# Routing by scattered token numbers, early blocks and one dispatch per expert in a linear-attention and expert kernel

## The chip, the cores and the metric

The kernel runs on one core of one Trainium2 chip. Its metric is the device time of one execution in microseconds (us). The engines are PE (matmul), DVE (vector), ACT (scalar), POOL (general purpose, and issuer of the indirect DMAs) and SP (issuer of plain DMAs). Each works through its own queue of instructions in order; semaphores order the queues against each other.

## The reference

A gated linear attention is followed by a mixture of eight experts, of which each token uses one.

```python
# attention: B, H, S, D = 4, 8, 768, 48, float32
for t in range(S):
    state = alpha[:, :, t, :, None] * state + np.einsum('bhd,bhde->bhde', k[:, :, t], v[:, :, t])
    y[:, :, t] = np.einsum('bhd,bhde->bhe', q[:, :, t], state)
x = y.transpose(0, 2, 1, 3).reshape(B * S, H * D)            # N = 3072 rows of 384
# router
xn = x / (norm(x) + 1e-6); en = expert_emb / (norm(expert_emb) + 1e-6)
logits = xn @ en.T / tau                                     # E = 8
expert_idx = np.argmax(logits, axis=1)
probs = softmax(logits)                                      # sum + 1e-9
gate_w = probs[np.arange(N), expert_idx]
# experts: w1 [8, 384, 1024], w2 [8, 1024, 384]
out[mask_e] = gate_w[mask_e, None] * (np.maximum(x[mask_e] @ w1[e], 0) @ w2[e])
```

## The kernel before

**Attention.** The 3072 tokens are 24 chunks of 128 (six for each of the four batches). The loop at the end of the attention part is written as a pipeline: in iteration s it loads chunk s + 2, takes the decays of chunk s (transposes on PE, two scans on DVE, `qs` on POOL), the scores of chunk s - 1, the mixing of chunk s - 2 and the rows of chunk s - 3. The function `rows` multiplies the transposed result with a selection matrix that also holds the expert embeddings, so that one PSUM tile `px` has a chunk's 384 values of x and its eight logits; ACT copies x out, DVE sums the logits, SP stores the 128 rows in the DRAM tensor `x_rows`, and ACT forms the sum of squares. The programs for the engines are put in order by a scheduler that follows the order of the program where an operation is ready, and it adds the waits. Each read of a tile or DRAM tensor waits for the writes that come before it in the program and touch the same part.

**Choosing an expert.** After each batch, `choose` scales the logits of six chunks (a square root and an exponential on ACT, eleven operations on DVE), marks the winning expert in `chosen` and adds up on POOL how often each expert was chosen before each chunk (`before`).

**Routing.** When the attention is over, the part with the lines 404 to 490 places all tokens at once: two matmuls rank every token within its expert (`rk`), DVE turns the ranks into a block number and a row, 24 matmuls of one-hot matrices (`in_row`, `inv`) invert that into the token number and the gate for each row of 31 possible blocks, and further DVE operations give the indices for gathering and scattering (`gidx`, `sidx`), each block's expert (`eblk`) and whether its weights have to be loaded (`fresh`).

**Experts.** `block` (line 506) handles 128 rows of one expert: it loads the expert's w1 and w2 into one of two buffers unless the block two before had the same expert, gathers the 128 rows of x with an indirect DMA (line 526), turns them with three PE transposes (536), runs the first layer as 24 matmuls with 128 moving columns (545) and ACT's ReLU, the second as 8 matmuls with 384 moving columns (555), multiplies by the gate on DVE (559) and scatters the rows to the output (560). A float32 matmul shows as two records in the profile, so that a block has 48 and 16 of them. Every expert's rows are filled up to whole blocks. The first 24 blocks are straight code. How many there are in all is known only at run time, so the last blocks are the arms of one dispatch (`Switch`, line 577): every engine loads the count into a register (`values_load`, line 573) and branches to its code of that arm. Each arm begins with a hint for its exit branch.

Of the kernel before, what the change touches and what calls it, by code (L numbers as in the profile page):

```python
# [9 lines left out]
FP32 = mybir.dt.float32  # L10
# [5 lines left out]
SP = mybir.EngineType.SP  # L16

# [6 lines left out]
def kernel(  # L24
# [24 lines left out]

    NBLK = (N + E * (P - 1)) // P  # L50
    FAR = 1 << 20

    x_rows = nc.dram_tensor("x_rows", (N, DM), FP32, kind="Internal").ap()
# [12 lines left out]
    zeros = consts.tile([P, P], FP32)  # L66
    nc.gpsimd.memset(zeros, 0.0)
    cols_i = consts.tile([P, P], I32)
    nc.gpsimd.iota(cols_i, pattern=[[1, P]], base=0, channel_multiplier=0)
    cols = consts.tile([P, P], FP32)  # L70
    nc.vector.tensor_copy(cols, cols_i)
    toks_i = consts.tile([P, NS], I32)
    nc.gpsimd.iota(toks_i, pattern=[[P, NS]], base=1, channel_multiplier=1)
    toks = consts.tile([P, NS], FP32)
    nc.vector.tensor_copy(toks, toks_i)
    first = consts.tile([P, E], FP32)
    nc.vector.tensor_scalar(first, cols[:, 0:E], -1.0, float(E), ALU.mult, ALU.add)


    lg = consts.tile([P, NS, E], FP32)  # L80
    sq = consts.tile([P, NS], FP32)
    gate = consts.tile([P, NS], FP32)
    chosen = consts.tile([P, NS, E], FP32)
    before = consts.tile([P, NS + 1, E], FP32)
    nc.gpsimd.memset(before[:, 0], 0.0)
    rtau = consts.tile([P, 1], FP32)
    gidx = consts.tile([P, NBLK], I32)
    sidx = consts.tile([P, NBLK], I32)
    bgate = consts.tile([P, NBLK], FP32)
    eblk = consts.tile([1, NBLK], I32)  # L90
    fresh = consts.tile([1, NBLK], I32)
    nmore = consts.tile([1, 1], I32)


    with ExitStack() as c1:
# [7 lines left out]
        NBUF, NBV = 4, 6  # L103
# [33 lines left out]
        sel = pads.tile([P, NP, 2 * D + E], FP32, name="sel")  # L137

        al0 = pads.tile([P, NP, NS], FP32, name="al0")

        def prepare():
# [15 lines left out]
            nc.vector.reciprocal(en, en)  # L157
            embp = work.tile([E, H, DP], FP32, name="embp", bufs=1)
# [23 lines left out]
        def choose(b):  # L182
            s0, s1 = b * NCH, (b + 1) * NCH
            shp = [P, NCH, E]
            l = lg[:, s0:s1]
            rn = work.tile([P, NCH], FP32, name="rn")
            nc.scalar.activation(rn, sq[:, s0:s1], AF.Sqrt)
            nc.vector.tensor_scalar(rn, rn, 1e-6, None, ALU.add)
            nc.vector.reciprocal(rn, rn)
            nc.vector.tensor_scalar(rn, rn, rtau, None, ALU.mult)  # L190
            nc.vector.tensor_tensor(l, l, bc(rn, shp, 2), ALU.mult)
            top = work.tile([P, NCH], FP32, name="top")
            nc.vector.tensor_reduce(top.unsqueeze(2), l, axis=AX.X, op=ALU.max)  # L193
            win = work.tile(shp, FP32, name="win")
            nc.vector.tensor_tensor(win, l, bc(top, shp, 2), ALU.is_equal)
            nc.vector.tensor_tensor(win, win, bc(first, shp, 1), ALU.mult)
            best = work.tile([P, NCH], FP32, name="best")
            nc.vector.tensor_reduce(best.unsqueeze(2), win, axis=AX.X, op=ALU.max)
            nc.vector.tensor_tensor(chosen[:, s0:s1], win, bc(best, shp, 2), ALU.is_equal)
            for s in range(s0, s1):  # L200
                nc.gpsimd.tensor_tensor(before[:, s + 1], before[:, s], chosen[:, s], ALU.add)
            sh = work.tile(shp, FP32, name="sh")
            nc.vector.tensor_tensor(sh, l, bc(top, shp, 2), ALU.subtract)
            nc.scalar.activation(sh, sh, AF.Exp)
            g = gate[:, s0:s1]
            nc.vector.tensor_reduce(g.unsqueeze(2), sh, axis=AX.X, op=ALU.add)
            nc.vector.tensor_scalar(g, g, 1e-9, None, ALU.add)
            nc.vector.reciprocal(g, g)
# [153 lines left out]
        def rows(s):  # L362
# [3 lines left out]
            for p in range(NP):  # L366
                nc.tensor.matmul(px[:, p], lhsT=yT[:, p], rhs=sel[:, p], start=True, stop=True)  # L367
            x = work.tile([P, NP, 2 * D], FP32, name="x", bufs=3)
            nc.scalar.copy(x, px[:, :, 0 : 2 * D])
            nc.vector.tensor_reduce(  # L370
                lg[:, s].unsqueeze(2), px[:, :, 2 * D :].rearrange("t p e -> t e p"),
                axis=AX.X, op=ALU.add,
            )
            xf = x.rearrange("t p d -> t (p d)")
            nc.sync.dma_start(out=x_rows[s * P : (s + 1) * P], in_=xf)
            x2 = work.tile([P, DM], FP32, name="x2")
            nc.scalar.activation(x2, xf, AF.Square, accum_out=sq[:, s : s + 1])
            if s % NCH == NCH - 1:
                choose(s // NCH)
# [22 lines left out]


    with ExitStack() as c2:
        rt = c2.enter_context(tc.tile_pool(name="rt", bufs=1))
        ps_rt = c2.enter_context(tc.tile_pool(name="ps_rt", bufs=1, space=PSUM))


        rk = ps_rt.tile([P, (NS + 1) * E], FP32, name="rk")
        nc.tensor.matmul(  # L410
            rk, lhsT=ones, rhs=before.rearrange("p s e -> p (s e)"), start=True, stop=False
        )
        nc.tensor.matmul(
            rk[:, 0 : NS * E], lhsT=earlier, rhs=chosen.rearrange("p s e -> p (s e)"),
            start=False, stop=True,
        )

        nb_i = rt.tile([P, E], I32, name="nb_i")
# [74 lines left out]
    with ExitStack() as c3:  # L493
# [77 lines left out]
        for j in range(NS):  # L571
            block(j)
# [37 lines left out]
```

## Time and profile before

| | us |
|---|---|
| median of three runs | 535.98 (533.46 to 536.34) |
| the profiled execution | 535.62 |
| its span, first to last instruction | 533.9 |
| PE busy, DVE busy | 464.1, 182.4 |
| last `px` of the attention ends | 162.0 |
| first expert matmul | 206.9 |
| last expert matmul ends | 523.8 |

The page of the profile has 40 equal slices of the span (13.3 us each), in which a digit is the busy share of an engine in tenths; PEclk is the clock that PE was granted, again in tenths. The chain of waits follows the work that ended last back through the program. A group line gives a line of the kernel, engine, operation, operands and shapes, then the number of instructions, their busy time, the mean of one in ns, and the idle time before them with what ended it. In a timeline the columns are start, duration, engine, line, operation. In the view of one source line, a name such as PEldq is the sequencer of that engine, the numbers after the count are the shortest, the median and the longest in ns, and then come the first and the last start.

### The profile page before, as it was taken

The numbers are of one execution on the slowest core, as the hardware profiler recorded it, in microseconds if no ns is written. First come the engines' busy times: TensorE is split into PE (matmuls) and PEld (weight loads), VectorE is DVE, ScalarE is ACT, GpSimd is POOL, SyncE is SP. The second block draws the span as 40 slices with busy tenths as digits, with TensorE's granted clock in tenths as the row PEclk, the third lists the DMA queues.
The fourth block names the chain that finished last, engine by engine and source line by source line (L and its number), as shares of the span: only waits on it lengthen the run. The fifth ranks groups of instructions, "written<-read, shape, count | busy, mean of one in ns | idle before, by whom it ended". The sixth has DMA issues, their size and how long they took to land.

```text
span 533.9 us, 9347 instructions
## 1 busy us (share of the span) xinstructions
PE 464.1 (87%) x3677; PEld 387.4 (73%) x3677; DVE 182.4 (34%) x391; ACT 111.2 (21%) x214; POOL 139.2 (26%) x224
## 2 busy tenths in 40 slices
PE   2999999999992636999999999999999999964992
PEld 2899889899891625778777787877778777743871
DVE  5888998998974710100101111010110101001000
ACT  2244544645543000101110001100001100000110
POOL 6554544553430132001202022020220200102000
PEclk9999999999997556999999999999999999995997
DMA  9889778777000078038477384086159295582000
GB/s 188 170 179 199 168 151 173 159 152 163 31 32 29 1 269 321 16 119 291 142 260 270 134 293 152 30 301 219 46 205 319 60 321 173 180 301 84 16 18 16
DMA packets 130229, 84.78 MB, mean 159 GB/s; under 512 B 102095, under 2 KB 121595, under 8 KB 130168
## 3 DMA queue, kind: packets, MB, share of 16 engines
q1 hardware_dynamic: 126336, 73.93, 48.2%
q0 software_dynamic: 3456, 10.03, 5.1%
q8 instruction: 32, 0.52, 0.4%
q14 instruction: 29, 0.24, 0.1%
q10 hardware_dynamic: 376, 0.05, 0.1%
HBM read 109.17 MB, written 10.03 MB: 223 GB/s over the span
## 4 chain that ended last, share of the span: by engine, by line
PE 73%; issue 10%; DVE 9%; DMA 4%; POOL 1%; another core or an unknown queue 1%; ACT 1%; POOLq 0%; ACTq 0%; DVEq 0%
PE ph L545 25%; PE pyo L555 23%; PE sc L328 4%; PE px L367 4%; PE py L342 3%; PE py L354 3%; DMA xg<-x_rows,gidx 2%; PE pkb L277 2%; PE inv L460 2%; PE pa L216 2%; PE pd L305 2%; DVE r L246 2%; PE pq L216 1%; PE pk L216 1%; DVE y L559 1%
## 5 line engine op out<-in xcount | busy, mean ns | idle before, releaser
L545 PEld LDWEIGHTS ph<-xgT,w 128*128 128x128 f32 x1296 | 150.9, 195 | 11.9 <-DVE xgT L538 4.9
L545 PE MATMUL ph<-xgT,w 128*128 128x128 f32 x1296 | 152.8, 279 | 5.5 <-DVE xgT L538 3.4
L555 PE MATMUL pyo<-w,hT 128*128 128x384 f32 x432 | 143.8, 486 | 0.0
L555 PEld LDWEIGHTS pyo<-w,hT 128*128 128x128 f32 x432 | 80.0, 190 | 50.1
L559 DVE TENSOR_SCALAR y<-pyo,bgate 128x384 f32<-128x384 f32 x27 | 16.7, 618 | 263.6 <-PE pyo L555 263.6
L551 ACT ACTIVATE hT<-ph 128x512 f32<-128x512 f32 x54 | 32.2, 597 | 320.5 <-PE ph L545 303.0
L560 POOL DMA_INDIRECT out_dram<-y,sidx x27 | 27.0, 1000 | 187.1 <-DVE y L559 184.7
L526 POOL DMA_INDIRECT xg<-x_rows,gidx x27 | 27.9, 1033 | 105.7 <-PE pxg L536 77.8
L268 POOL TENSOR_TENSOR qs<-qc,a 128x512 f32<-128x512 f32 x24 | 30.6, 1274 | 48.9 <-DVE a L260 30.9
L536 PE MATMUL pxg<-ident,xg 128*128 128x128 f32 x81 | 14.8, 319 | 27.3 <-DMA xg<-x_rows,gidx 18.8
L536 PEld LDWEIGHTS pxg<-ident,xg 128*128 128x128 f32 x81 | 10.9, 162 | 33.3 <-issue 30.5
L332 DVE TENSOR_TENSOR sm<-sc,causal 128x512 f32<-128x512 f32 x48 | 30.6, 674 | 0.5 <-PE sc L328 0.4
L246 DVE TENSOR_TENSOR_SCAN r<-pa,inr 128x511 f32<-128x511 f32 x24 | 29.3, 1220 | 3.6 <-PE pa L216 3.1
L260 DVE TENSOR_TENSOR_SCAN a<-pa,ini 128x512 f32<-128x512 f32 x24 | 29.4, 1223 | 1.2
L328 PE MATMUL sc<-qs,kr 64*128 64x128 f32 x384 | 28.6, 289 | 0.0
L538 DVE COPY xgT<-pxg 128x384 f32<-128x384 f32 x27 | 14.1, 551 | 41.7 <-PE pxg L536 23.3
L328 PEld LDWEIGHTS sc<-qs,kr 64*128 64x128 f32 x384 | 24.0, 192 | 4.1 <-issue 1.9
L289 POOL TENSOR_TENSOR dec<-state,end 64x256 f32<-64x256 f32 x40 | 24.4, 609 | 7.0 <-DVE top L193 1.9
L367 PE MATMUL px<-sel,yT 128*128 128x104 f32 x192 | 25.3, 275 | 0.7 <-ACT yT L360 0.7
L354 PE MATMUL py<-sm,vt 128*64 128x128 f32 x384 | 25.3, 274 | 0.0
L367 PEld LDWEIGHTS px<-sel,yT 128*128 128x128 f32 x192 | 23.3, 192 | 1.3 <-ACT yT L360 0.9
L360 ACT COPY yT<-py 128x512 f32<-128x512 f32 x24 | 14.1, 586 | 37.8 <-PE py L354 37.8
(127 smaller groups left out, 391.9 us busy)
## 6 DMA issues: line engine op xcount, KB each, us to landing
w<-in_moe_w_dram SPq DMA_DIRECT2D x54, 1536.0 KB
at<-in_alpha_dram SPq DMA_DIRECT2D x24, 192.0 KB
kt<-in_k_dram SPq DMA_DIRECT2D x24, 192.0 KB
qt<-in_q_dram SPq DMA_DIRECT2D x24, 192.0 KB
vt<-in_v_dram SPq DMA_DIRECT2D x24, 192.0 KB
x_rows<-x SPq DMA_DIRECT2D x24, 192.0 KB
xg<-x_rows,gidx POOLq DMA_INDIRECT x27, 4.6
out_dram<-y,sidx POOLq DMA_INDIRECT x27, 6.1
```

What stands on the lines that cost most here:

```text
L246: nc.vector.tensor_tensor_scan(r[:, L - 2 :: -1], pa[:, L - 1 : 0 : -1], inr[:, L - 2 :: -1], 1.0, ALU.mult, ALU.add,)
L260: nc.vector.tensor_tensor_scan(a, pa, ini, 0.0, ALU.mult, ALU.add)
L268: nc.gpsimd.tensor_tensor(qs.rearrange("p n t -> p (n t)"), qc, a, ALU.mult)
L328: nc.tensor.matmul(sc[:, hh, p], lhsT=kr[sl, p], rhs=qs[sl, p], start=True, stop=True)
L332: nc.vector.tensor_tensor(sm[:, hh], sc[:, hh], causal.to_broadcast([P, NP, P]), ALU.mult)
L354: nc.tensor.matmul(py[DP * hh : DP * hh + DP, p], lhsT=vt[:, 2 * p + hh], rhs=sm[:, hh, p], start=("dec" not in d and p == 0), stop=True, ...
L367: nc.tensor.matmul(px[:, p], lhsT=yT[:, p], rhs=sel[:, p], start=True, stop=True)
L526: nc.gpsimd.indirect_dma_start(out=xg, out_offset=None, in_=x_rows, in_offset=bass.IndirectOffsetOnAxis(ap=gidx[:, j : j + 1], axis=0), bo ...
L545: nc.tensor.matmul(ph[:, f], lhsT=w1_t[:, i, (f0 + f) * P : (f0 + f + 1) * P], rhs=xgT[:, i], start=(i == 0), stop=(i == KT - 1),)
L551: nc.scalar.activation(hT[:, f0 : f0 + 4], ph, AF.Relu)
L555: nc.tensor.matmul(py, lhsT=hT[:, f], rhs=w2_t[:, f], start=(f == 0), stop=(f == FT - 1))
L560: ins = nc.gpsimd.indirect_dma_start(out=out, out_offset=bass.IndirectOffsetOnAxis(ap=sidx[:, j : j + 1], axis=0), in_=y, in_offset=None, ...
```

## The change

- `choose` is replaced by `place`, called after each of seven groups of chunks (5, 5, 5, 5, 2, 1 and 1). It marks the winner from unscaled logits, ranks the group's tokens with two matmuls, and for each chunk scatters 128 token numbers (plus one) with an indirect DMA from POOL into a DRAM tensor `ids`, which has 3072 places per expert and starts with zeros. The whole routing part after the attention goes.
- The logits and the sum of squares are stored with each row of x, 393 values a row, by ACT instead of SP. The gate is computed from them for the gathered rows (`gates`).
- After 20 chunks, `first_expert` takes the first expert that has at least 256 rows. The experts are then done in turn from it. Its first two blocks are done ahead of all others, from token numbers read in `ids` and rows of the first 20 chunks.
- `counts` gives the rest of each expert's rows in halves of 64, and each expert has one dispatch with an arm for 0 to 8 halves, and one with a loop over blocks for more. In an arm the first layer takes all rows of the expert at once as moving columns (up to 512). The second layer of a last half block uses two matmuls with 64 weight columns, which write different halves of a PSUM tile and are added afterwards.
- Within the arm of one expert the rows of the next one are turned, always four blocks. Weights have three buffers, gathered rows three; weights and rows are fetched two experts ahead, before the dispatch.
- The buffers of v go from six to five.

```diff
-    x_rows = nc.dram_tensor("x_rows", (N, DM), FP32, kind="Internal").ap()
+    GROUPS = ((0, 5), (5, 10), (10, 15), (15, 20), (20, 22), (22, 23), (23, 24))
+    S0, EARLY = 20, 2
+    x_rows = nc.dram_tensor("x_rows", (N, ROW), FP32, kind="Internal").ap()
+    ids = nc.dram_tensor("ids", ((E * NB + NB) * P, 1), I32, kind="Internal").ap()
+    id_blocks = ids.rearrange("(j p) one -> p (j one)", p=P)
...
+    def weights(i):
+        e = nc.values_load(
+            turn_i[0:1, i : i + 1], engines=(SP,), min_val=0, max_val=E - 1,
...
+        nc.sync.dma_start(
+            out=w1_s[i % NW], in_=w1_r[ds(e, 1)].rearrange("e p k f -> (e p) k f")
+        )
...
-        NBUF, NBV = 4, 6
+        NBUF, NBV = 4, 5
...
+        def place(g):
+            nc.vector.tensor_reduce(top.unsqueeze(2), l, axis=AX.X, op=ALU.max)
+            nc.vector.tensor_tensor(win, l, bc(top, shp, 2), ALU.is_equal)
+            nc.vector.tensor_tensor(win, win, bc(first, shp, 1), ALU.mult)
+            nc.vector.tensor_reduce(best.unsqueeze(2), win, axis=AX.X, op=ALU.max)
+            nc.vector.tensor_tensor(ch, win, bc(best, shp, 2), ALU.is_equal)
             for s in range(s0, s1):
+                (nc.vector if s == NS - 1 else nc.gpsimd).tensor_tensor(before[:, s + 1], before[:, s], chosen[:, s], ALU.add)
+            rk = ps_mm.tile([P, GMAX, E], FP32, tag="mm", name="rk")[:, 0:n]
+            nc.tensor.matmul(
+                rkf, lhsT=ones, rhs=before[:, s0:s1].rearrange("p s e -> p (s e)"),
+                start=True, stop=False,
+            )
+            nc.tensor.matmul(
+                rkf, lhsT=earlier, rhs=ch.rearrange("p s e -> p (s e)"),
+                start=False, stop=True,
+            )
+            nc.vector.tensor_tensor(at, rk, ch, ALU.mult)
+            nc.vector.tensor_reduce(row.unsqueeze(2), at, axis=AX.X, op=ALU.add)
+            nc.vector.tensor_copy(dest[:, s0:s1], row)
+            for s in range(s0, s1):
+                ins = nc.gpsimd.indirect_dma_start(
+                    out=ids,
+                    out_offset=bass.IndirectOffsetOnAxis(ap=dest[:, s : s + 1], axis=0),
+                    in_=toks[:, s : s + 1],
...
+                tc.declare_no_dep(ins.ins, group="ids", reason="tokens have a row each")
+                tc.add_to_no_dep_group("ids", ins.ins)
...
             nc.vector.tensor_reduce(
+                l.unsqueeze(2), px[:, :, 2 * D :].rearrange("t p e -> t e p"),
                 axis=AX.X, op=ALU.add,
             )
-            nc.sync.dma_start(out=x_rows[s * P : (s + 1) * P], in_=xf)
+            nc.scalar.copy(x[:, LG : LG + E], l)
+            nc.scalar.copy(x[:, 0:DM].rearrange("t (p d) -> t p d", p=NP), px[:, :, 0 : 2 * D])
+            nc.scalar.activation(x2, x[:, 0:DM], AF.Square, accum_out=x[:, SQ : SQ + 1])
+            nc.scalar.dma_start(out=x_rows[s * P : (s + 1) * P], in_=x)
+            if s == s1 - 1:
+                place(g)
+                if s1 == S0:
+                    first_expert()
+                if s1 == NS:
+                    counts()
...
-    with ExitStack() as c2:
...
+        def gates(xg, gate, n):
+            nc.vector.tensor_reduce(top.unsqueeze(2), l, axis=AX.X, op=ALU.max)
+            nc.scalar.activation(rn, xg[:, :, SQ : SQ + 1], AF.Sqrt)
...
+            nc.scalar.activation(sh, sh, AF.Exp)
+            nc.vector.tensor_reduce(gate.unsqueeze(2), sh, axis=AX.X, op=ALU.add)
...
+        def first_layer(w1_t, hT, xT, f, n):
+            ph = ps_h.tile([P, NC * P], FP32, name="ph")[:, 0:n]
+            for i in range(KT):
+                nc.tensor.matmul(
+                    ph, lhsT=w1_t[:, i, f * P : (f + 1) * P], rhs=xT[:, i, 0:n],
+                    start=(i == 0), stop=(i == KT - 1),
+                )
+            nc.scalar.activation(hT[:, f, 0:n], ph, AF.Relu)
...
+        def second_layer(w2_t, hT, t, n, gate, col):
...
+                for f in range(FT // 2):
+                    for i in range(2):
+                        nc.tensor.matmul(
+                            py[i * HALF : (i + 1) * HALF],
+                            lhsT=hT[:, i * FT // 2 + f, t * P : t * P + HALF],
+                            rhs=w2_t[:, i * FT // 2 + f],
+                            start=(f == 0), stop=(f == FT // 2 - 1), skip_group_check=True,
+                        )
+                nc.scalar.copy(y[0:HALF], py[HALF:])
+                nc.vector.tensor_tensor(y[0:HALF], y[0:HALF], py[0:HALF], ALU.add)
+                nc.vector.tensor_scalar(y[0:HALF], y[0:HALF], gate[0:HALF], None, ALU.mult)
+            scatter(y[0:n], col[0:n])
...
+        def rows_of(i, m, ready=None):
+            hT = hp.tile([P, FT, NC * P], FP32, name="hT") if m else None
+            for f in range(FT):
+                if m:
+                    first_layer(w1_t, hT, xT, f, m * HALF)
+                if i + 1 < E and f % 2 == 1:
+                    prepare(i + 1, f // 2)
+            if i + 1 < E:
+                gates(xg_s[(i + 1) % NXG], gt_s[(i + 1) % 2], NC)
+            for t in range((m + 1) // 2):
+                second_layer(
+                    w2_t, hT, t, min(P, m * HALF - t * P), gt[:, t : t + 1],
+                    sidx[:, i, t : t + 1],
+                )
...
+        nc.sync.dma_start(out=etok, in_=id_blocks[:, ds(lead * NB, EARLY)])
+        for i in range(2):
+            weights(i)
+        tokens_of(etok, egidx, esidx, EARLY)
+        for t in range(EARLY):
+            gather(exg[:, t], x_rows[0 : S0 * P], egidx[:, t : t + 1])
+        for t in range(EARLY):
+            turn(exg[:, t], exT[:, :, t * P : (t + 1) * P])
+        gates(exg[:, 0:EARLY], egt[:, 0:EARLY], EARLY)
+        hT = hp.tile([P, FT, NC * P], FP32, name="hT")
+        for f in range(FT):
+            first_layer(w1_s[0], hT, exT, f, EARLY * P)
+        for t in range(EARLY):
+            if t == EARLY - 1:
+                for i in range(E):
+                    nc.sync.dma_start(out=tok[:, i], in_=id_blocks[:, ds(first_block(i), NC)])
...
+                for i in range(2):
+                    gathers(i)
+                for b in range(NC):
+                    prepare(0, b)
+                gates(xg_s[0], gt_s[0], NC)
+            second_layer(w2_s[0], hT, t, P, egt[:, t : t + 1], esidx[:, t : t + 1])
+        for i in range(E):
+            if i + 2 < E:
+                weights(i + 2)
+                gathers(i + 2)
+            count = nc.values_load(
+                halves[0:1, i : i + 1], min_val=0, max_val=2 * NC + 1,
...
+            for m in tc.Switch(count, 2 * NC + 2):
+                if m <= 2 * NC:
+                    rows_of(i, m)
+                else:
+                    many(i)
```

## The prediction

> **What bounds the kernel now.** First the slices of the span and the busy times by stage: is there one bound or several?
>
> ```profile
> PE   2999999999992636999999999999999999964992
> PEclk9999999999997556999999999999999999995997
> ```
>
> ```profile
> core 0: us, PE busy (x) PEld busy (x) DVE busy (x) ACT busy (x) POOL busy (x), PEclk, DMA share, GB/s
> 93.00:130.00 37.00, 36.47 (x460) 33.55 (x459) 33.71 (x66) 19.24 (x40) 19.10 (x35) 1.00 0.77 164
> ...
> 162.00:206.80 44.80, 16.19 (x67) 14.11 (x68) 17.92 (x69) 4.11 (x7) 10.49 (x14) 0.54 0.38 141
> 206.80:475.50 268.70, 263.12 (x1595) 209.03 (x1593) 24.16 (x45) 28.66 (x48) 40.80 (x41) 0.99 0.56 192
> 475.50:490.90 15.40, 2.43 (x10) 1.72 (x11) 1.73 (x3) 0.00 (x0) 4.04 (x4) 0.64 0.52 166
> ```
>
> PE bounds the attention (36.5 of 37 us, DVE close behind with 33.7) and the experts (263 of 269). Between them lie 44.8 us with PE a third busy at half clock, and 15.4 us more open up near the end. The chain of waits says what fills the first hole:
>
> ```profile
> 162.03 0.49 ACT x L369
> ...
> 178.00 10.52 PE inv L460 x48
> ...
> 191.38 6.62 DMA xg<-x_rows,gidx
> ...
> 199.40 6.68 DMA xg<-x_rows,gidx
> ...
> 207.08 6.82 PE ph L545 x48
> 213.90 5.16 PE pyo L555 x16
> 219.06 5.36 PE ph L545 x48
> ```
>
> Routing ends at 189.2, and then PE waits for gathers. The transposes of blocks 1 to 4 stand ahead of block 0's first layer on PE's queue, so that layer starts at 206.9 though block 0's rows were there at 197. The second hole is the one dispatch (Switch) of before; the lines of its source and of its timeline show it:
>
> ```profile
> L573 PEldq TENSOR_LOAD <-nmore x1: 483/483/483, 471.0 to 471.0; - x1
> ```
>
> ```profile
> L577 PEldq BRANCH_PREFETCH_HINT  x1: 50/50/50, 477.7 to 477.7; - x1
> ```
>
> ```profile
> L605 PEldq COMPARE_BRANCH  x2: 342/3078/5814, 471.8 to 519.3; - x2
> ```
>
> ```profile
> 470.13 5.33 PE L555 MATMUL pyo<-w,hT 128*128 128x384 f32 x16
> ...
> 484.37 1.05 POOL L526 DMA_INDIRECT xg<-x_rows,gidx  x1 [7.00 <-DMA xg<-x_rows,gidx]
> ```
>
> PE's sequencer reads the count at 471.00, while 4.45 us of issued matmuls still run (to 475.45), and the branch holds it 5.81 us: the arm's first instruction comes at 477.72. So a dispatch costs PE itself 2.3 us; the other 10 of the hole are POOL's branch (476.93 to 482.60) and gathers issued only behind it. The exit branch took PE 0.34, and its next instruction followed at 0.46.
>
> Costs of one instruction:
>
> ```profile
> L545 PE MATMUL ph<-xgT,w 128*128 128x128 f32 x1296 | 152.8, 279 | 5.5 <-DVE xgT L538 3.4
> L555 PE MATMUL pyo<-w,hT 128*128 128x384 f32 x432 | 143.8, 486 | 0.0
> ...
> L560 POOL DMA_INDIRECT out_dram<-y,sidx x27 | 27.0, 1000 | 187.1 <-DVE y L559 184.7
> L526 POOL DMA_INDIRECT xg<-x_rows,gidx x27 | 27.9, 1033 | 105.7 <-PE pxg L536 77.8
> ```
>
> The means are latencies; in the chain 16 second-layer records take 5.17 us (0.323 each, 0.841 ns a column) and 48 first-layer ones 5.36 (0.112, 0.873 ns a column).
>
> **The attention.** Removed: three calls of choose inside the loop (the fourth is in the hole). The scans of L246 start 8.7, 8.0 and 7.9 us apart there against 5.8 elsewhere: 7.2 us. Added: four calls of place in the loop, each with 8 small DVE operations (0.2 to 0.23 and a gap: 1.9 us, on a nearly full DVE), 4 matmul records behind POOL's adds, and 5 scatters on POOL. Scatters cost what L560 does, 1.0 us at a distance of 1.3: a burst of 6.5 us on an engine in order, with qs (L268) and dec (L289) queued behind it, and PE's scores and DVE's state waiting for those. qs has 1.4 us of slack (ends at 87.8, scores from 89.2) and POOL idles about 2 us a chunk before it; over two chunks they absorb 5.4 and leave 1.1. With 0.5 for the matmuls a place costs 3.5, four of them 14. Bounds: 1.9 each (all POOL work hidden) to 10.7 (6.5 + 1.35 of adds + 1.0 + 1.9, nothing hidden). The logits now reach x by an ACT copy that waits for DVE, and the store moves from SP to ACT's queue (issues of 0.27 to 0.62 us there at the start): ACT is half busy, so 0 to 0.3 us a chunk, taken 0.1, together 2.4. One v buffer fewer costs nothing while loads run two chunks ahead: PE never waits for a load in the attention. Sum: 14 + 2.4 - 7.2 = +9; bounds 0 to +43. The last chunk's px ends at 171 instead of 162.0.
>
> **From there to the first layer.** Now 44.9 us. After: six DVE operations 1.4, rank matmuls 0.6, three operations 0.7; the last scatter, landing 2.6 to 6.1 us after issue (L560's rows), taken 4.0 as the queues are emptier; the read of two id blocks on SP, which depends on every scatter (no size of it is in the trace; from 0 up to a gather's 4.6), taken 2.0; three operations 0.7; two gathers 1.6 to the second's issue, landing 3.0 to 6.6 (L526), taken 4.0; transposes and copy 1.5. Together 16.5 (bounds 11 to 24). The first expert is known three chunks earlier, so weights (3 MB, at the 300 GB/s of the slices 10 us) can be on their way, and hide under these waits; if they queue behind the id read they arrive 5 us after it, still in time. First layer from 187.5.
>
> **The experts.** The reference's inputs give the experts 418, 365, 379, 426, 395, 371, 351 and 367 tokens: 27 blocks before. After 20 chunks expert 0 has 337, so it leads, and the rest is 3, 6, 6, 7, 7, 6, 6, 6 halves: 51 with the four early ones. First layer: 48 records of 64 columns a half at 0.841 ns, 2.585 us, 131.8 (at 0.873 it is 137). Second: 24 full blocks of 5.17, 124.1; three half blocks whose two 64-column matmuls go at once. That they do is seen in the attention: 16 such records (L354) take 1.02 us, 8 full-width ones (L342) 1.09. So 2.6 each, 7.8 (15.5 if not). Transposes: four blocks for every expert, full or not, 32 of 0.41: 13.1 (six records take 0.82). The restart at half clock costs 1.3. Sum 278.1.
>
> **Eight dispatches.** PE's path is load 0.48, registers 0.37, branch 5.81, 0.06: 6.72, less the issued work. The first: 2.3. After a full block, with the exit's 0.46: 2.7, four times. After a half block the same 14 issued matmuls last half as long, 2.25: 4.9, and there the clock falls (in the trace it fell 3.65 and 4.2 us after PE stopped, and the next 48 matmuls took 6.7 to 6.8 instead of 5.4): 6.2, three times. Sum 31.7. Bounds: 0 (a branch of 0.34 would hide under the issued work) to 10.5 each (nothing issued ahead, ACT's exit of 2.4, cold clock). I take the same construct's own row.
>
> The Trainium skill (Advanced Engine Details and Errata, Control Flow Timing) gives about 108 ns for a compare-and-branch; by that the dispatches would cost nothing and the sum below would be 32 lower. Its page Runtime: NRT & Kernel Launch (Instruction fetch mechanics) speaks against the change: a taken branch whose target isn't loaded stalls for a fetch. The 5.81 us row is of that kind, so the measurement decides.
>
> **What is covered.** Id reads for all experts, 8 gathers and expert 0's transposes need 19 us behind the last scatter's landing; the early blocks' work ends 31 behind it. Weights of the expert after next have a body of some 35 us. POOL pays per expert four gathers 5.2, scatters 4, paddings of the DMA counts about 5 (0.72 and a wait each), exit and branch 9: 23 of 35. DVE enters an arm 9.5 us after its last y; the third transposed block needs it 9 to 14 us into the arm. ACT's gates (two table loads, 1.28 each) lie beside the second layer. The end stays 10.1 us.
>
> **The sum.** 187.5 + 278.1 + 31.7 + 10.1 = 507.4; outside the span 535.62 - 533.9 = 1.7: 509.1. The profiled execution (535.62) stands 0.4 below the median shown (535.98), so nothing is added.
>
> **Rivals.**
> Dispatch dominates (slower): every gap goes to the upper bound, 84 instead of 31.7, because PE's issued work no longer covers and weight loads slow the fetch: 561. It decides from 7.3 us a gap on. For: eight cold branches on five engines. Against: PE's own gap was 2.3.
> POOL's bursts bound the attention: +36 instead of +9, 536, no change. For: POOL in order, slack of 1.4. Against: POOL is half busy.
> The early blocks don't wait for the last scatters and run beside the last chunks: 16 earlier, when expert 0's rows become the limit: 493. For: their x rows are cut to the first 20 chunks. Against: the ids they read are one tensor that every scatter writes.
> PE's queue order puts expert 0's transposes ahead of the early first layer, as it did with blocks 1 to 4: the cover is lost, +12: 521.
>
> **How the numbers follow.** Forecast 0.56, dispatch 0.13, bursts 0.10, earlier 0.12, order 0.09. Half a per cent (2.7 us) is about what a measurement can tell from no change. Faster: forecast, earlier, order and a third of bursts, 0.80; same 0.06 from bursts; slower, dispatch and a little of bursts, 0.14. The range goes from the earlier case with a cheaper attention, 487, to where dispatch passes before, 541.
>
> **What would show it.** Right: no inv matmuls; the last px near 171; ph at 256 columns from about 187; 48 ph records in 15.5 us for six halves; PE gaps of 2 to 6 us at eight places. Wrong: gaps over 7 us, DVE or PE waiting for qs and dec after each place by more than 5 us, PE waiting for gathers before an arm's transposes, or the last scatter's landing late.

## The result, and the profile after

The changed kernel takes 599.95 us (median of four, 596.96 to 603.28) against 534.86 for the kernel before on the same chip: a ratio of 1.122, with a 95% interval of 1.114 to 1.129. The prediction was 509.1 with a range of 487 to 541. The profiled execution took 596.96 with a span of 595.2.

By stages (windows that end at the first place, the last `px`, the first `ph`, the transposes of expert 0 ahead of the first dispatch, the last matmul of all, and the end of the span; times busy in us, the count of records in brackets, then the granted clock):

```profile
core 0: us, PE busy (x) PEld busy (x) DVE busy (x) ACT busy (x) POOL busy (x), PEclk, DMA share, GB/s
20.00:56.00 36.00, 34.95 (x440) 32.06 (x436) 31.74 (x56) 14.89 (x36) 18.37 (x30) 1.00 1.23 186
56.00:234.10 178.10, 127.10 (x1366) 116.29 (x1366) 94.96 (x201) 48.71 (x121) 74.85 (x119) 0.85 0.51 79
234.10:256.40 22.30, 2.82 (x13) 1.98 (x11) 4.57 (x29) 2.68 (x6) 3.40 (x4) 0.53 0.47 170
256.40:285.50 29.10, 24.90 (x92) 17.90 (x92) 3.84 (x13) 4.21 (x10) 8.48 (x9) 0.91 0.87 266
285.50:581.90 296.40, 264.20 (x868) 154.70 (x868) 41.95 (x119) 52.95 (x99) 49.33 (x50) 0.95 0.28 90
581.90:595.20 13.30, 0.04 (x1) 0.00 (x0) 0.62 (x1) 0.00 (x0) 0.97 (x1) 0.69 0.04 15
```

Until 56 us PE is full as before. From the first place on it works 127 of 178 us, at a clock of 0.85. The slices of the span show the same as holes behind each of the four places of five chunks:

```profile
PE   2998469849829837087778997979889979989991
PEclk9999869889869978579698999999979979999997
```

Against the kernel before and the prediction (first scan is the first scan of DVE, L246 before and L356 after; it starts at 11.5 to 13.7 us, differently from run to run, so the attention is measured from it):

| us | before | predicted | after |
|---|---|---|---|
| first scan to the end of the last `px` | 150.5 | 159.5 | 220.8 |
| from there to the first first-layer matmul | 44.9 | 16.5 | 22.3 |
| first to last expert matmul | 316.9 | 309.8 | 325.5 |
| last matmul to the end | 10.1 | 10.1 | 13.3 |

Of the 88 us between forecast and result, 61 lie in the attention, 6 in the stage behind it, 16 in the experts and 3 at the end; the first scan came 2 late. What PE waits for in the attention is named by the waits (window 55 to 236 us: engine, line and tile, what was waited for, sum, times, longest):

```profile
PE py L452 <- POOL dec L399: 41.9, 4, 12.9
...
POOL dec L399 <- DMA ids<-toks,dest: 34.4, 3, 12.4
DVE state L427 <- POOL dec L399: 24.7, 3, 11.9
...
PE rk L249 <- POOL before L246: 7.6, 5, 1.8
```

POOL's own sequence behind the first place shows how:

```profile
59.53 1.19 POOL L263 DMA_INDIRECT ids<-toks,dest  x1 [0.95 <-DVE dest L261]
61.02 0.97 POOL L263 DMA_INDIRECT ids<-toks,dest  x1 [0.30 <-issue]
62.30 0.97 POOL L263 DMA_INDIRECT ids<-toks,dest  x1 [0.30 <-issue]
63.57 0.97 POOL L263 DMA_INDIRECT ids<-toks,dest  x1 [0.30 <-issue]
64.85 0.97 POOL L263 DMA_INDIRECT ids<-toks,dest  x1 [0.30 <-issue]
65.83 0.23 POOL L373 TENSOR_TENSOR end<-r,al 128x4 f32<-128x4 f32 x1
65.98 0.63 POOL L399 TENSOR_TENSOR dec<-state,end 64x256 f32<-64x256 f32 x1
78.96 0.61 POOL L399 TENSOR_TENSOR dec<-state,end 64x256 f32<-64x256 f32 x1 [12.34 <-DMA ids<-toks,dest]
79.65 1.28 POOL L378 TENSOR_TENSOR qs<-qc,a 128x512 f32<-128x512 f32 x1
```

The burst of five scatters lasts 6.3 us, as the prediction had it. Then the second of the two `dec` instructions waits 12.3 us for their landing, though it touches neither `ids` nor `dest`. In the trace it waits on the semaphores of all five scatters; the first half, on partitions 0 to 63, waits for none, and the second, which starts at partition 64, does. Why only the second carries them is not shown. In the kernel before the two halves of a chunk run back to back, and the longest wait of either in the loop is 1.8 us, for DVE behind a call of choose:

```profile
93.89 1.29 POOL L289 TENSOR_TENSOR dec<-state,end 64x256 f32<-64x256 f32 x2
```

Behind the waiting half stand `qs` and the mixing matmuls. A scatter takes a median of 10.3 us from issue to landing here.

### The profile page after: what moved, and what is told of

The parts are those of the page before. It is cut to its first block, busy times and chain, and to the rows that moved or that the text cites. A ratio compares the mean times of both kernels' runs of the same rounds, so it can differ in the third digit from the quotient of the medians.

```text
span 595.2 us, 7919 instructions
## 1 busy us (share of the span) xinstructions
PE 462.4 (78%) x2814; PEld 330.2 (55%) x2814; DVE 188.2 (32%) x453; ACT 128.6 (22%) x279; POOL 166.3 (28%) x252
## 5 line engine op out<-in xcount | busy, mean ns | idle before, releaser
L594 PE MATMUL ph<-xT,w 128*128 128x384 f32 (+3 forms) x432 | 148.1, 499 | 32.9 <-issue 19.3
L594 PEld LDWEIGHTS ph<-xT,w 128*128 128x128 f32 x432 | 84.8, 204 | 86.1 <-issue 45.9
L606 PE MATMUL pyo<-w,hT 128*128 128x384 f32 x384 | 125.5, 486 | 0.0
L606 PEld LDWEIGHTS pyo<-w,hT 128*128 128x128 f32 x384 | 72.4, 190 | 48.5
L452 PE MATMUL py<-qs,dec 128*128 128x128 f32 x160 | 26.8, 321 | 41.9 <-POOL dec L399 41.9
L610 DVE TENSOR_SCALAR y<-pyo,gt 128x384 f32<-128x384 f32 x24 | 14.8, 618 | 132.4 <-PE pyo L606 132.3
L598 ACT ACTIVATE hT<-ph 128x384 f32<-128x384 f32 (+3 forms) x72 | 31.9, 472 | 77.9 <-PE ph L594 77.8
L452 PEld LDWEIGHTS py<-qs,dec 128*128 128x128 f32 x160 | 23.8, 229 | 43.7 <-POOL dec L399 42.9
L532 POOL DMA_INDIRECT xg<-x_rows,gidx x32 | 32.2, 1006 | 33.5 <-issue 17.4
L571 DVE COPY xT<-pxg 128x384 f32<-128x384 f32 x34 | 18.2, 549 | 58.0 <-PE pxg L570 57.9
L356 DVE TENSOR_TENSOR_SCAN r<-pa,inr 128x511 f32<-128x511 f32 x24 | 29.3, 1220 | 6.7 <-PE pa L326 6.7
L263 POOL DMA_INDIRECT ids<-toks,dest x24 | 23.7, 986 | 14.9 <-DVE dest L261 6.1
## 6 DMA issues: line engine op xcount, KB each, us to landing
x_rows<-x ACTq DMA_DIRECT2D x24, 196.5 KB, 11.5
```

The costliest lines, as they stand in the source:

```text
L356: nc.vector.tensor_tensor_scan(r[:, L - 2 :: -1], pa[:, L - 1 : 0 : -1], inr[:, L - 2 :: -1], 1.0, ALU.mult, ALU.add,)
L452: nc.tensor.matmul(py[:, p], lhsT=dec[:, p].rearrange("p j e -> p (j e)"), rhs=d["qs"][:, p], start=(p == 0), stop=False, skip_group_check ...
L532: nc.gpsimd.indirect_dma_start(out=xg, out_offset=None, in_=src, in_offset=bass.IndirectOffsetOnAxis(ap=col, axis=0), bounds_check=src.sha ...
L594: nc.tensor.matmul(ph, lhsT=w1_t[:, i, f * P : (f + 1) * P], rhs=xT[:, i, 0:n], start=(i == 0), stop=(i == KT - 1),)
L598: nc.scalar.activation(hT[:, f, 0:n], ph, AF.Relu)
L606: nc.tensor.matmul(py, lhsT=hT[:, f, t * P : (t + 1) * P], rhs=w2_t[:, f], start=(f == 0), stop=(f == FT - 1),)
```

## Experiments

The expectations call 236 us the last `px` of the changed kernel; that is the end of the routing's last matmul, and the `px` itself ends at 234.1. Ratios are to the kernel before on the same chip, with 95% intervals.

| run | median us | ratio | first scan to last px | px to first layer | experts |
|---|---|---|---|---|---|
| changed kernel | 599.95 | 1.122 (1.114 to 1.129) | 220.8 | 22.3 | 325.5 |
| dec_one_op | 578.21 | 1.075 (1.069 to 1.082) | 192.2 | 19.9 | 330.9 |
| one_scatter_a_chunk | 573.67 | 1.068 (1.062 to 1.074) | 192.2 | 22.6 | 331.5 |
| scatters_late | 587.32 | 1.097 (1.093 to 1.100) | 167.9 | 60.9 | 328.0 |
| ids_64_bytes | 546.52 | 1.020 (1.016 to 1.025) | 171.0 | 16.0 | 330.8 |
| ids_64_bytes_two_dec | 554.53 | 1.033 (1.028 to 1.037) | 179.6 | 16.4 | 332.1 |
| ranks_one_chunk_later | 530.87 | 0.991 (0.988 to 0.994) | 163.9 | 19.1 | 324.3 |
| norm_in_attention | 519.35 | 0.970 (0.968 to 0.973) | 160.4 | 17.8 | 311.6 |

### The wait of dec

```diff
-            for hh in range(2):
-                sl = slice(DP * hh, DP * hh + DP)
-                nc.gpsimd.tensor_tensor(
-                    dec[sl, :, hh], carried["state"][sl],
-                    d["end"][sl].to_broadcast([DP, NP, DP]), ALU.mult,
-                )
+            shp = [P, NP, 2, DP]
+            nc.gpsimd.tensor_tensor(
+                dec, bc(carried["state"], shp, 2), bc(d["end"], shp, 3), ALU.mult,
+            )
```

`end` gets a second column per head pair, with a factor `al1` that is zero for the other half of the partitions.

> The changed kernel with one edit: dec is computed by one POOL instruction on 128 partitions (its factor end holds zeros for the other half) instead of two on 64, so that no POOL instruction of the attention starts at partition 64, and dec no longer waits for the landing of earlier scatters. The scatters, their number and their place in POOL's order stay. Theory (dec's wait for the landing is the loss): the four gaps of PE before the mixing matmuls (12.9, 6.1, 12.5, 10.4 us, 41.9 together) shrink to 3 or less each, and with them the stretches at half clock (54.6 us in the attention), so that the last px ends at 170 to 185 us instead of 236, and the time is 535 to 555. Rival (five scatters in a row hold POOL, or their traffic holds the other transfers): the gaps move to qs or to the next memset but stay, the last px ends after 220 and the time is 580 to 600.

Measured: 578.21 us, the last `px` at 205.6. The attention loses 28.6 us (220.8 to 192.2), and the waits for the scatters' landing are gone. But both theories missed: the stage is still 33 us above the forecast, and the wait has another form. Two views of the trace show it, first POOL's longest wait from 20 to 206 us, then SP's issues behind the first place (start, duration):

```profile
POOL at L342 <- DMA at<-in_alpha_dram: 37.0, 8, 8.0
```

```profile
62.82 0.37 SPq L340 DMA_DIRECT2D at<-in_alpha_dram  x1
63.67 0.38 SPq L343 DMA_DIRECT2D kt<-in_k_dram  x1
64.15 3.68 SPq L344 DMA_DIRECT2D qt<-in_q_dram  x1
67.93 5.86 SPq L345 DMA_DIRECT2D vt<-in_v_dram  x1
73.89 2.17 SPq L340 DMA_DIRECT2D at<-in_alpha_dram  x1
76.15 4.17 SPq L343 DMA_DIRECT2D kt<-in_k_dram  x1
```

While scatters are on their way SP needs 3.7 and 5.9 us to issue one load of 192 KB (0.4 to 1.5 between 56 and 150 us in the kernel before). The alpha loads are late, and the memset of `at`, which stands in POOL's queue ahead of `dec`, waits for them. So the scatters slow the loads too.

> The kernel before with the same edit of dec alone, as a control. Two instructions of 0.61 us become one like qs (128x512, 1.27 us), so the edit by itself should be worth 0: 533 to 538 by the theory and by the rival. Faster by 10 us or more would mean that the edit removes something else than a wait for scatters.

Measured: 537.65 us, ratio 1.004 (1.001 to 1.007). Inside what was expected: the edit alone brings nothing without scatters; it costs 2 us.

### Scatters outside the attention

```diff
-            for s in range(s0, s1):
+        def send():
+            nc.vector.tensor_copy(dest2, dest)
+            for s in range(NS):
                 ins = nc.gpsimd.indirect_dma_start(
                     out=ids,
-                    out_offset=bass.IndirectOffsetOnAxis(ap=dest[:, s : s + 1], axis=0),
+                    out_offset=bass.IndirectOffsetOnAxis(ap=dest2[:, s : s + 1], axis=0),
...
                 if s1 == NS:
+                    send()
                     counts()
```

> The changed kernel with all 24 scatters issued after the last group's row numbers (they read a copy of these, made there), none in the attention. What is left of place in the loop is the marking, the adding up, the rank matmuls and the logits' way into x. Theory: the last px ends at 165 to 185 us as in the run with one dec instruction, because without scatters nothing is waited for; the scatters then lie bare behind it, 24 x 1.3 = 31 us instead of 1.3, so the first layer starts 45 to 55 us behind the last px and the time is 560 to 580. If place's other parts are the loss (rank matmuls, ACT's copy that waits for DVE), the last px still ends after 215 and the time passes 600.

Measured: 587.32 us. The last `px` ends at 181.3, as expected without any wait for scatters. So marking, ranks and the logits' new way into x cost 167.9 - 150.5 = 17.4 us, net of what the removal of choose gives back. The time itself was missed because the scatters took longer than their issue. Here they run with next to no other traffic (the rate of all DMA in that time rounds to 0 GB/s); the read of the early ids (`etok`, on SP) waits for the last landing:

```profile
184.36 1.18 POOL L267 DMA_INDIRECT ids<-toks,dest  x1 [4.59 <-DVE halves L318]
185.85 0.97 POOL L267 DMA_INDIRECT ids<-toks,dest  x1 [0.30 <-issue]
...
199.94 0.96 POOL L267 DMA_INDIRECT ids<-toks,dest  x1 [1.68 <-DMA ids<-toks,dest]
...
219.65 0.97 POOL L267 DMA_INDIRECT ids<-toks,dest  x1 [0.30 <-issue]
```

```profile
230.84 0.39 SPq L691 DMA_DIRECT2D etok<-ids  x1
```

From 184.4 to 230.8 that is 46.4 us for 24 scatters of 512 bytes, 1.9 us each, though POOL can issue one in 1.27.

### Spread, or wider

Two theories for the slow loads: the burst of five, or the small writes themselves.

```diff
+        later = {S0: (15, 16), S0 + 1: (17, 18), S0 + 2: (19,)}
+        for j in range(S0 - 5):
+            later[j + 5] = (j,)
...
+            for j in later.get(s, ()):
+                send(j, s)
```

> The run with one dec instruction, with the scatters of a group of five spread over the next five chunks, one a chunk (the row numbers of a chunk are rounded by a small DVE instruction in the later chunk; the last groups as before), so that no more than two follow each other. Theory C (it is the burst of five in a row that holds POOL 6.5 us and starves the loads): one scatter of 1.3 us fits into POOL's idle 2 us a chunk, the waits of the memset for alpha fall below 12 us, the last px ends at 181 to 190 instead of 206, and the time is 545 to 558. Rival D (every scatter takes its 2 to 4 us from the loads wherever it stands): the loads are late a little in each chunk, the last px ends at 198 to 210 and the time stays at 565 to 585.

Measured: 573.67 us, with the last `px` at 205.8: rival D. Spreading moves the waits (19.2 us of the memset for alpha, 24.6 us of the rank matmuls for POOL's adds, 9.6 the longest) and gains nothing in the attention.

```diff
-    ids = nc.dram_tensor("ids", ((E * NB + NB) * P, 1), I32, kind="Internal").ap()
+    ids = nc.dram_tensor("ids", ((E * NB + NB) * P, W), I32, kind="Internal").ap()    # W = 16
...
-                    in_=toks[:, s : s + 1],
+                    in_=toks_w[:, s],                  # the token number 16 times
```

> The run with one dec instruction, with places of 64 bytes instead of 4 in ids: each scatter writes 128 pieces of 64 bytes (16 copies of the token number, of which the first is read), and the zeros at the start are nine DMAs of 197 KB. In the run with all scatters late, 24 of them took 46.4 us from the first issue to the last landing with no other traffic (1.9 us each for 0.5 KB, while POOL could issue one in 1.27). Theory A (writes of 4 bytes are what is slow, and what slows the loads beside them): the waits of POOL's memset for the alpha load (37 us with 4 bytes) fall below 12, the last px ends at 183 to 193 instead of 206, and the time is 545 to 560. Rival B (any indirect DMA of 128 pieces beside the loads costs the same): the waits stay above 25 us, the last px ends at 200 to 210, the time stays at 570 to 585.

Measured: 546.52 us, the last `px` at 182.7: theory A. Five scatters in a row are still there, and cost 171.0 - 167.9 = 3.1 us against none in the loop. The loads behind the first place are issued in 0.4 to 1.1 us, the memset waits 0.8 us in all, and the DMA list (55 to 200 us; median time to landing last) has:

```profile
x_rows<-x ACTq DMA_DIRECT2D x19, 196.5 KB, 3.2
ids<-xg,dest POOLq DMA_INDIRECT x24, 2.2
```

In the changed kernel's list the same two stand at 15.5 and 10.3 us:

```profile
x_rows<-x ACTq DMA_DIRECT2D x15, 196.5 KB, 15.5
ids<-toks,dest POOLq DMA_INDIRECT x15, 10.3
```

The 64-byte places alone, with `dec` left in two instructions:

> The changed kernel with places of 64 bytes in ids as its only edit; dec stays two instructions, of which the second still waits for the landing of the group's five scatters. Theory (scatters of 4 bytes are the cause, dec's wait only one of the ways in which their slowness reaches PE): with landings of 2.2 us, as in the run with 64 bytes and one dec, the wait costs POOL about 2 us a group, 4 groups 8 at most; the last px ends at 183 to 192 us and the time is 546 to 557. Rival (dec's wait costs by itself, however fast the scatters are): four gaps of 6 us or more stay at PE's mixing matmuls, the last px ends after 205 and the time is 570 or more.

Measured: 554.53 us, the last `px` at 191.5. The wait of `dec` is worth 8.6 us (179.6 - 171.0) when scatters land in 2.2 us, and 28.6 when they take 10. It carries the slowness of the scatters to PE; it isn't the root.

### Size of a write, or its neighbours

A chunk's tokens of one expert get places next to each other, so with 4-byte places up to 16 writes of one scatter fall into the same 64 bytes.

```diff
-                    in_=toks_w[:, s],
+                    in_=toks[:, s : s + 1],            # ids is flat again, dest times 16
```

> The run with one dec instruction and places of 64 bytes, but each scatter writes only the first 4 bytes of a place (row numbers times 16), so that the writes are as small as in the changed kernel and no two of them fall into the same 64 bytes. If the size of a write is what is slow: scatters land late and the loads starve as in the run with 4-byte places, the last px ends at 198 to 210 us and the time is 568 to 584. If it is that neighbouring tokens of an expert write into the same 64 bytes: as fast as with 64-byte writes, landing 2 to 3 us, last px at 180 to 188, time 543 to 552.

Measured: 552.36 us, ratio 1.029 (1.023 to 1.035), the last `px` at 187.3. Both stand at the upper bound of what the neighbour theory expected. With writes as small as before, the last scatter lands within 2.3 us (the early ids are read at 192.3, the scatter was issued at 190.0; with 4-byte places 5.7 in the run with one `dec` and 7.3 in the changed kernel), and the memset waits 0.3 us for alpha. The semaphore records put the landings of its scatters at 2.0 to 4.9 us, against 4.0 to 16.0 with 4-byte places and one `dec`. Of the 0.055 in ratio between the 4-byte and the 64-byte places, 0.046 come from the distance alone; in the attention it is 16.8 of 21.2 us (192.2 to 175.4, and to 171.0).

> The run with one dec instruction and places of 32 bytes, all written: twice two neighbours in 64 bytes. If the size of a write is what counts, something between: by size alone half way, 552 to 570. If sharing 64 bytes counts and 32 bytes is written whole: pairs of neighbours still share, and the time is between 546 and 572 as well, but the landing of a scatter is nearer to the 10 us of the 4-byte one than to 2.2. If neither matters from 32 bytes on: landing 2 to 3 us, time 543 to 552.

Measured: 555.10 us, ratio 1.035 (1.030 to 1.041), the last scatter landing within 2.3 us and all of them in 1.9 to 4.9. So a distance of 32 bytes is enough for quick landing; two writes may share 64 bytes. Distances between 4 and 32 bytes were not run. The time itself lies outside the 543 to 552 of "neither matters" and inside the range of the theory on size. Why this run and the last are 9 and 6 us behind full 64-byte writes stays open: in the attention the scan distance at the fourth place is longer (13.8 and 13.3 against 10.8 us), with no wait for loads, and the experts took 336.2 and 335.0 us against 330.8.

### What the removed call of choose was worth

```diff
-            if s % NCH == NCH - 1:
-                choose(s // NCH)
+            if s == NS - 1:
+                nc.vector.tensor_copy(sq2, sq)
+                for b in range(B):
+                    choose(b)
```

> The kernel before with its four calls of choose all made after the last chunk (they read a copy of the sums of squares, made there), to measure what the three calls in the loop cost. The prediction gave the change 7.2 us for their removal, read from the distance of three scans (8.7, 8.0, 7.9 against 5.8): by that the last px ends at 155 instead of 162.0. Rival: PE is the bound of the attention (6.24 us of records for a full chunk, 5.3 for the first and last of a batch, 35.5 for six, and six chunks took 36.4 with choose), DVE only lags for a chunk and PE catches up: each call costs 1, and the last px ends at 159 to 161. The time of the whole is 537 to 546 by both, because three more calls then stand in the hole behind the attention.

Measured: 538.54 us, ratio 1.006 (1.004 to 1.008); the last `px` at 160.6 with a first scan 2.0 later, so the attention takes 147.2 instead of 150.5. Three calls are worth 3.3 us, not 7.2. The rival is right: after each long distance the scans of before follow at 5.7 instead of 6.2, PE catching up.

### The dispatches

```diff
-            count = nc.values_load(
...
-            for m in tc.Switch(count, 2 * NC + 2):
-                if m <= 2 * NC:
-                    rows_of(i, m)
-                else:
-                    many(i)
+            rows_of(i, (3, 6, 6, 7, 7, 6, 6, 6)[i])
```

> The changed kernel with the eight dispatches taken out: the arm of each expert is fixed when the program is built, by the counts of this input (3, 6, 6, 7, 7, 6, 6, 6 halves), and no count is read. It leaves out the choice at run time. The dispatches' visible gaps on PE were 21.7 us, the starts of arms behind ACT and DVE 10.6, and four stretches at half clock followed (30.7 us, worth some 10 to 15). If all of it is the dispatches', the time falls by 32 to 47: 550 to 565. If only the gaps themselves are, by 22: 575. If straight code waits for its instructions just as long, it stays near 597. The attention stays as it is, with its last px near 236.

Measured: 563.42 us, ratio 1.048 (1.041 to 1.054). The expert part falls from 325.5 to 295.5, 30.0 us, and the end from 13.3 to 9.7, with the attention as slow as in the changed kernel. The first expectation held. The Trainium skill (Advanced Engine Details and Errata, Control Flow Timing) gives about 108 ns for a compare-and-branch; by an estimate from it eight of them would be worth 1 us. The run without them disagrees.

### A version that is faster than both

The rank matmuls of a group wait 1.8 to 2.2 us for POOL's adds, and DVE behind them. Issued one chunk later, they find these done:

```diff
+            if s == s0 and g > 0:
+                rank(g - 1)
+                if s0 == S0:
+                    first_expert()
+                    for i in range(2):
+                        weights(i)
             if s == s1 - 1:
                 place(g)
...
                 if s1 == NS:
+                    rank(g)
                     counts()
```

> The run with one dec instruction and 64-byte places, with two more edits: the rank matmuls and what follows them are issued one chunk after the marking and adding up of a group (so PE doesn't wait for POOL's adds at them), and the weights of the first two experts are loaded as soon as the order of the experts is known, ahead of the read of the early ids instead of behind it. A place still cost 3.8 us of scan distance in the run with 64 bytes. Theory (PE's waits of 1.8 to 2.2 us for POOL's adds, and DVE's for the ranks behind them, are what a place costs when scatters are quick; DVE's eight small operations are caught up): 2.5 to 3 us of each of four places and 1 of two small ones go, the last px ends at 168 to 173 instead of 182.6, the first layer starts 13 to 15 us behind it instead of 16.2, and the time is 530 to 537. Rival (DVE's own time for place is the cost): the last px stays at 179 to 183, the time at 540 to 546.

Measured: 530.87 us, ratio 0.991. The attention gains 7.1 us; the last `px` ends at 175.6, 2.6 later than expected. The first layer starts 19.1 us behind it, not 13 to 15: the earlier weights bring nothing, and the ranks of the last but one group now stand behind the last `px`. The last scatter, with the weights on their way beside it, is read after 5.6 us (178.6 to 184.2) instead of 2.3; whether the weights slow it was not tested. And with PE's waits for POOL's adds gone the bursts show, which the prediction had priced: PE's scores wait 8.4 us for `qs` over the four places.

```diff
+            nc.scalar.activation(x[:, SQ : SQ + 1], x[:, SQ : SQ + 1], AF.Sqrt)
             nc.scalar.dma_start(out=x_rows[s * P : (s + 1) * P], in_=x)
...
-            nc.scalar.activation(rn, xg[:, :, SQ : SQ + 1], AF.Sqrt)
-            nc.vector.tensor_scalar(rn, rn, 1e-6, None, ALU.add)
+            nc.vector.tensor_scalar(rn, xg[:, :, SQ : SQ + 1], 1e-6, None, ALU.add)
```

> The run before this one with one more edit: the square root of the sum of squares is taken by ACT in the attention and stored with the row, so that the gates of the experts need no square root, and ACT keeps one table in the experts (one table load instead of two for every expert). PE waited 10 to 11 us in all at the starts of arms for hT from ACT, which enters an arm with a table load of 1.28 us and a square root that waits for the gathered rows, ahead of its first relu. If that is why ACT is late, most of these 10 us go: 521 to 530. If ACT is late because of its own branch, 1 to 3 us go. The 24 more small operations on ACT (0.2 us each) lie in the attention beside PE.

Measured: 519.35 us, ratio 0.970 (0.968 to 0.973), a little better than expected. Waits of PE at the starts of arms, in the run before (first) and in this one:

```profile
PE ph L618 <- ACT hT L622: 15.4, 7, 4.9
```

```profile
PE ph L618 <- ACT hT L622: 5.4, 3, 2.7
```

And ACT's table loads from 190 to 582 us in the run before, of which this one has none in that window:

```profile
L609 ACT ACT_TABLE_LOAD x9 | 11.5, 1283 | 60.9 <-DVE gsh L608 60.9
L603 ACT ACT_TABLE_LOAD x8 | 10.3, 1283 | 59.6 <-issue 44.2 <-DMA xg<-x_rows,gidx 15.3
```

The experts take 311.6 instead of 324.3 us, of which 10.0 are these waits. Another 3.5 in the attention weren't expected and stay open.

## Why the prediction was wrong

**The step that failed** is the price of a place, "Scatters cost what L560 does, 1.0 us at a distance of 1.3", with the attention's "Sum: 14 + 2.4 - 7.2 = +9; bounds 0 to +43". The attention took 70.3 us more, outside the bounds. They counted what a scatter takes of POOL's time, never what waits for its landing inside the loop, nor what it takes from the loads. The prediction's own sign of being wrong came: PE waited 41.9 us for `dec` over the four places, more than 5 at each. The landing times of L560 (2.6 to 8.0 us) were used for the last scatter alone. In the runs' numbers, from 150.5 us on:

| part | predicted | measured | from |
|---|---|---|---|
| choose leaves the loop | -7.2 | -3.3 | choose_late |
| marking, ranks, logits into x | with the next | +20.7 | scatters_late, less choose |
| five scatters in a row on POOL | +16.4 in all | +3.1 | ids_64_bytes against scatters_late |
| 4-byte places instead of 64-byte ones | not there | +21.2, of which 16.8 by the distance | dec_one_op against ids_64_bytes and ids_4_of_64_bytes |
| dec's wait for landings of 10 us | not there | +28.6 | changed kernel against dec_one_op |

The working is a chain of single steps: run by run, not each taken alone. The same wait costs 8.6 with quick landings. Steps that also put `dec` into one instruction hold the cost of that edit, which was 1.3 us of the attention in the kernel before (150.5 to 151.8).

Two terms inside the bounds were mis-sized as well. A place without scatters cost 3.3 to 3.8 us of scan distance (9.6 and 10.0 against 6.2 at the first three in scatters_late), the size foreseen, but not made up as foreseen: PE waits 1.8 us there for POOL's adds, and DVE then for the ranks. Ranks a chunk later took 7.1 us of the attention away. What the rest of the 20.7 is was not taken apart; a granted clock of 0.96 instead of 1.00 over that attention is some 14 us at half speed and can hold up to 7 of it, by an estimate from these clocks. The two small groups placed after 22 and 23 chunks, also in the loop, were left out of "four calls". And choose was read from single long distances, without the shorter ones that followed them.

**The rival "POOL's bursts bound the attention"** came nearest, but its mechanism is not what made the loss: the burst, without slow landings, is worth 3.1.

**To the first layer** 22.3 instead of 16.5, inside the bounds of 11 to 24. The last scatter's landing took 7.3 (237.2 to 244.5) instead of 4.0. With 64-byte places, where it took 2.3, the stage measured 16.0. That the early blocks wait for the last scatters was right.

**Dispatches.** The mechanism and the size were right: 31.7 predicted, 30.0 in the run without them. PE's eight branches into an arm took 3.4 to 6.6 us (5.81 was taken), its exits 0.3. The three gaps behind experts with a last half block are 5.1 to 5.4 us, where 4.9 and a slow clock were foreseen. PE's waits from 285 to 582 us:

```profile
PE ph L594 <- issue: 19.3, 4, 5.4
PE ph L594 <- ACT hT L598: 10.6, 5, 3.6
...
PE ph L594 <- DVE y L610: 2.4, 2, 1.3
```

The visible gaps between arms were 21.7 (3.6, 5.4, 1.3, 1.1, 5.1, 5.2, and two hidden), and 10.6 more came as PE's waits for `hT`, since ACT enters an arm late. These aren't all the dispatches' own: 5.2 of such waits stand in the run without dispatches too, and moving the square root took 10.0 of 15.4 away with the dispatches in place (norm_in_attention). The prediction had put ACT "beside the second layer", which the scheduler's order of ACT's queue didn't keep: its table load and square root stand ahead of the first relu. "Dispatch dominates" did not come.

**Experts** took 325.5 instead of 309.8. The forecast of 278.1 without dispatches compares with 295.5 in the run without them. Named are a wait of 4.2 for the first gathered rows, which was called covered, and ACT's entry. The clock is part of the rest: means of 0.91 and 0.95 in the two windows of the experts are some 35 us at half speed, which take up to 17, and the forecast had 5.2 (four times 1.3).

**Expert 0's transposes** did not come ahead of the early first layer, so the rival "PE queue order" fell. The **end** took 13.3 instead of 10.1; without dispatches it was 9.7, so the exit of the last arm is in it.

## What to carry to other kernels

Price an indirect DMA three times: the issuing engine's time, the landing that something later may wait for, and what it takes from other transfers. Look in the built order for waits that later instructions of the issuing queue carry on it without sharing data. Give scattered small values places at least 32 bytes apart (shorter distances above 4 were not run). A stall on an engine with slack costs less than the longest distance shows: count over the chunks that follow too.

## What the hardware showed that was not expected

- 128 writes of 4 bytes into neighbouring places took 1.9 us a scatter with next to nothing beside them; in the attention the median landing was 10 us, and one load's issue on SP rose from 0.4 to 1.1 us to as much as 5.9. At a distance of 32 or 64 bytes the scatters landed in 1.9 to 5.0 us and the last one within 2.3, whether 4 or 64 bytes were written (ids_64_bytes, ids_4_of_64_bytes, ids_32_bytes).
- The waits stop PE long enough to cost its clock: granted 0.85 from 56 to 234 us in the changed kernel, 1.00 in the same work before.
- ACT's 17 table loads in the experts (1.28 us each), on an engine that is busy a fifth of the time, cost PE: without them and the square roots the experts took 12.7 us less.
